# A new order for the first eight periods of an attention kernel: its second period's first scores in two more PSUM banks, seventeen dummy transposes left out

## The chip, the cores and the metric

The kernel runs on one core of one Trainium2 chip. The metric is the device time of one execution in microseconds (us); lower is better. Times are medians of several runs. The engines are TensorE (PE, with its weight loads shown apart as PEld), VectorE (DVE), ScalarE (ACT), GpSimd (POOL) and SyncE (SP), which issues every DMA of the kernel. Each engine takes its instructions strictly in the order in which the program lists them; between engines, semaphores say when data is ready or a buffer is free.

## The reference, cut to what matters

The kernel computes three things in a row: attention with a mask, a mixing layer, and an MLP. Only the start of the attention is touched by what follows.

```
q_bits = (einsum('bhsd,dk->bhsk', q, proj) > 0)      # 6 bits per token and head
k_bits = (einsum('bhsd,dk->bhsk', k, proj) > 0)
mask   = q_bucket[..., :, None] == k_bucket[..., None, :]   # buckets: the bits as a number
scores = where(mask, scale * q @ k.T, -1e9)
attn   = exp(scores - max); attn = attn / (sum(attn) + 1e-9)
x      = attn @ v                                   # 2 x 8 heads, 768 tokens, 64 per head
# then: theta = x @ w_theta; token mixing; channel mixing; norm; MLP with 4 x 512 columns
```

Everything is float32. Each operand of a product is split into a high part, rounded to the narrower fp32r form, and a low part, the rest; a product is then high by high, low by high and high by low.

## The kernel before

**Periods.** The attention has 16 heads of 768 tokens. A head's 768 query rows are six blocks of 128. The work goes in 48 periods of two row blocks: period p, block i (0 or 1) belongs to head (2p+i)//6, so head 0 is periods 0 to 2, head 1 is periods 3 to 5, and so on. One block's scores are a 128 x 772 tile `s` that fills two PSUM banks (two halves of 386 columns). In one period, with the letters that the order is written in:

- S (`s_mm`, L332): the scores of one block, four matmuls of 386 columns from the stacked tiles `tq`, `tk` (high parts, and the low parts below them) and `tq2`, `tk2` (high by low, with the bits of the mask as 7 more rows). For periods 0 to 2 there is no stack yet, and D (`direct_mm`, L503, six matmuls) and Q (`direct_bits`, L515, two) do the same from the split tiles themselves.
- M (`s_max`, DVE L340) takes the row maximum, E (`s_exp`, ACT L356) the exponential with its sum, tb (POOL L347) and R2 (DVE L363) what the norm needs, n (`s_norm`, POOL L367) normalizes into `pn`.
- U (`p_transpose`, PE L380): twelve 128 x 128 transposes, in three PSUM banks T0, T1, T2. H (`p_hi`, ACT L389) and L (`p_lo`, DVE L101) split them into `pth` and `ptl`.
- PV (`pv_mm`, PE L405): twelve matmuls into bank O; O and X (ACT L414, DVE) take the result out.

**PSUM.** There are eight banks: T0, T1, T2 and O, one each, and S0 and S1, two each. Block 0 of every period uses S0, block 1 uses S1. So D of period 1, block 0, waits until E of period 0, block 0 has read S0.

**Bits.** ac, ay, ab, aw make the mask bits of the first pair of heads; bc (PE L286, six matmuls of 384 columns), by (ACT L304), bb (DVE L310), bw make those of the next three pairs, in four chunks that use T2 and O in turn.

**Loads and splits.** SP loads the raw k and q of a pair of heads (lr, L166), v (lv, L174, the tile `vs`) and `gT` (gl, L654), and copies split tiles into the stacks of a head (sk, six DMAs, L248 to L253; sb, two for the bits, L647, L648). ACT splits off high parts (sh: `hik`, `hiq`, L210), DVE and POOL low parts (sl: `lok`, `loq`). vh (ACT L94) makes the high part of `vs` in two halves, into `vv`; vl the low part. At most eight of SP's DMAs are under way: the trace shows SP's issue of one waiting for the DMA issued eight places earlier.

**Dummies.** `warm` is a tile that nobody reads. Twelve matmuls of 384 columns write it at the start (L549), and seventeen transposes of the identity (L493) between the scores of period 0 and those of period 1.

**What sets the order.** The text `head` lists the operations of the first eight periods one by one; from period 8 on, the tables `plan` and `plan_b` and the dictionaries `bg`, `bg2`, `bg3` (background work by period) make the order. An operation's place in that list is its place on its engine. So one engine does not see how far the others have come, except where it waits for them.

Of the kernel before, what the change touches and what calls it, by code (L numbers as in the profile page):

```python
# [9 lines left out]
F32 = mybir.dt.float32  # L10
# [5 lines left out]
PSUM = bass.MemoryType.PSUM  # L16
# [17 lines left out]
def attn_moe_kernel(  # L34
# [35 lines left out]

    def bank(tag, name):
        return psum.tile([128, 512], F32, tag=tag, name=name)
# [360 lines left out]
    def theta_steps(c, x, y):  # L433

        r = slice(256 * x, 256 * x + 256)
        o = {}

        def s():
            if "h" not in WA:
                WA["h"] = const.tile([128, 4, 512], F32R, tag="wAh", name="thh")  # L440
                WA["l"] = const.tile([128, 4, 512], F32R, tag="wAl", name="thl")
            o["t"] = conv_tiles(ap_, th_st[c, x])
            conv_s(*o["t"])

        return (
            (at, 0, s), (at2, y, lambda: conv_y(*o["t"])), (at3, 1, lambda: conv_low(*o["t"])),
            (at3, 1 + y, lambda: conv_join(*o["t"])), (at2, 1 + y, lambda: cast(act, WA["h"][:, c, r], o["t"][1])),
            (at, 2 + y, lambda: sub(pool, WA["l"][:, c, r], o["t"][1], WA["h"][:, c, r])),
        )

    order.enter_context(tc.manual_schedule())

    plan = (
        ("Sa", 0), ("U0", 2), ("L2", 3), ("nb", 2), ("Ma", 0), ("H0", 2), ("X", 4), ("D", 0),
        ("R2", 1), ("U1", 2), ("Sb", 0), ("Mb", 0), ("H1", 2), ("U2", 2), ("Ea", 0), ("ta", 0), ("H2", 2),
        ("G", 0), ("na", 1), ("PV", 3), ("tb", 0), ("Eb", 0), ("L0", 2), ("C", 0), ("L1", 2), ("O", 3),
    )

    plan_b = (
        ("Sa", 0), ("B1", 2), ("L2", 3), ("B2", 2), ("U0", 2), ("Ma", 0), ("H0", 2), ("B3", 2),  # L460
        ("Sb", 0), ("ta", 0), ("nb", 2), ("X", 4), ("R2", 1), ("Ea", 0), ("Mb", 0), ("U2", 2), ("G", 0),
        ("U1", 2), ("H1", 2), ("H2", 2), ("L0", 2), ("C", 0), ("PV", 3), ("L1", 2), ("na", 1), ("B4", 2),
        ("Eb", 0), ("O", 3), ("tb", 0),
    )

# [29 lines left out]
    def direct_mm(p, i):  # L495

        ps = psum.tile([128, 2, 512], F32, tag=f"S{i}", name=f"s{p}_{i}")
        s_ps[p, i] = ps
        r = slice((2 * p + i) * 128, (2 * p + i + 1) * 128)
        K, kk = (64, [hl["k", 0, y] for y in (0, 1)]) if p == 0 else (128, kz)  # L500
        for x, y in ((0, 0), (0, 1), (1, 0)):
            for hf in range(2):
                pe.matmul(  # L503
                    ps[:, hf, 0:HW], hl["q", 0, x][0:K, r],
                    kk[y][0:K, hf, :], start=(x + y == 0), stop=False,
                )
# [41 lines left out]
    for x in range(12):  # L548
# [5 lines left out]
    TS = tuple(range(22, 46, 3))  # L554
    bg, bg2, bg3 = {}, {}, {}

    def at(step, fn, *args):
        bg.setdefault(step, []).append((fn, args))

    def at2(step, fn, *args):  # L560
        bg2.setdefault(step, []).append((fn, args))

    def at3(step, fn, *args):
        bg3.setdefault(step, []).append((fn, args))


    for h in range(5, B * H):
        at({8: 20}.get(h, 3 * h - 7), stack_dma, h)
        at({8: 21, 9: 21}.get(h, 3 * h - 7), stack_bits, h)
    v_steps = {2: (6, 9, 10), 3: (15, 16, 18), 4: (20, 22, 23)}  # L570
    for n in range(2, NPAIR):
        ld, *hi = v_steps.get(n, (6 * n - 6, 6 * n - 3, 6 * n - 2))
        at(ld, load_v, n)
        for x in range(2):
            at2(hi[x], v_hi, n, act, x)
            at(hi[x] + 1, v_lo, n, pool, x)
    for n, ld in ((6, 8), (7, 13)):
        at(ld, load_raw, n)
    for nm, n, *hi in (
        ("k", 5, 7, 11), ("q", 5, 8, 9), ("k", 6, 12, 13), ("k", 7, 14, 15),  # L580
        ("q", 6, 16, 17), ("q", 7, 17, 18),
    ):
        for x in range(2):
            at2(hi[x], split_hi, nm, n, act, x)
            at(hi[x] + 1, split_lo, nm, n, pool, x)
    for i in range(8):
        c, x = divmod(i, 2)
        at(TS[i] - 2 if i < 2 else max(TS[i] - 3, TS[i - 2] + 2), theta_load, c, x)
        for slot, d, fn in theta_steps(c, x, int(i < 7)):
            slot(TS[i] + d, fn)  # L590
# [18 lines left out]
    for step, fn, j, a in (  # L609
        (30, z_hi, 0, 0), (31, z_hi, 0, 1), (32, z_lo, 0, 0), (32, z_lo, 0, 1),  # L610
        (33, z_hi, 1, 0), (36, z_hi, 1, 1), (37, z_lo, 1, 0), (38, z_lo, 1, 1),
        (38, z_hi, 2, 0), (39, z_hi, 2, 1), (43, z_lo, 2, 0), (44, z_lo, 2, 1),
    ):
        at(step, fn, j, a)
# [3 lines left out]

    def run_bg(q):
        def run(p):  # L620
            for fn, args in q.pop(p, []):
                fn(*args)
        return run

    ops = {
        "Sa": lambda p: s_mm(p, 0), "Sb": lambda p: s_mm(p, 1),
        "Ma": lambda p: s_max(p, 0), "Mb": lambda p: s_max(p, 1),
        "ta": lambda p: None, "tb": s_lone,
        "Ea": lambda p: s_exp(p, 0), "Eb": lambda p: s_exp(p, 1),
        "R2": s_recip, "na": lambda p: s_norm(p, 0), "nb": lambda p: s_norm(p, 1),  # L630
        "B1": lambda p: bits_chunk(*bq[p], "T1"), "B2": lambda p: bits_y_(*bq[p]),
        "B3": lambda p: bits_b_(*bq[p]), "B4": lambda p: bits_p_(*bq[p]),
        "PV": pv_mm, "O": pv_evac_a, "X": pv_evac_b,
    }
    for u in range(3):
        ops[f"U{u}"] = lambda p, u=u: p_transpose(p, u)
        ops[f"H{u}"] = lambda p, u=u: p_hi(p, u)
        ops[f"L{u}"] = lambda p, u=u: p_lo(p, u)
    K0 = 8
    nxt = {op: K0 - d for op, d in plan}  # L640

# [11 lines left out]
    def g_load():  # L653
        sp.dma_start(out=gT, in_=g_ln.rearrange("(c p) -> p c", p=128))  # L654

# [6 lines left out]
    def bp_(x, e):  # L662
# [9 lines left out]
    hops = dict(  # L672
# [11 lines left out]
        n=s_norm, U=p_transpose, H=p_hi, L=p_lo, PV=pv_mm, O=pv_evac_a, X=pv_evac_b,  # L684
    )

    head = """
        sh.k.0.0.0 pb.0.0 pb.0.2 sl.k.0.0.0 pb.0.1 sh.k.0.1.0 sl.k.0.1.0 sh.q.0.0.0 sl.q.0.0.0 sh.q.0.1.0 ac.0
        sl.q.0.1.0 fk ac.1 ay.0 ay.1 kz.1.1 ac.2 ay.2 D.0.0 ab.0 lr.3.0 ab.1 ac.3 sh.k.1.2.0 D.0.1 ay.3 ab.2
        sh.q.1.2.0 aw.0.1 aw.1.1 pb.1.0 aw.2.0 kz.0.0 ab.3 Q.0.0 M.0.0 Q.0.1 warm.17 pb.1.2 E.0.0 lr.3.1 M.0.1  # L690
        sl.q.1.2.1 E.0.1 pb.1.1 D.1.0 sl.k.1.2.0 sh.k.3.2.0 Q.1.0 tb.0 lr.2.0 R2.0 lr.2.1 aw.3.0 M.1.0 n.0.1
        sk.1 sh.k.2.2.0 D.1.1 n.0.0 E.1.0 U.0.2 Q.1.1 U.0.0 sh.q.3.2.0 sl.k.2.2.0 sl.k.3.2.0 U.0.1 sl.q.3.2.1
        H.0.0 D.2.0 M.1.1 H.0.2 bc.0.1 L.0.2 L.0.0 Q.2.0 sh.q.2.2.0 E.1.1 M.2.0 by.0 tb.1 H.0.1 bc.1.0 D.2.1
        lv.0 bb.0 sl.q.2.2.1 L.0.1 by.1 sb.1 R2.1 Q.2.1 bw.0.1 n.1.0 E.2.0 bb.1 vh.0.0 lr.4.0 bc.3.1 M.2.1
        vh.0.1 S.3.0 lr.5.0 vl.0.0.0 bc.2.0 by.3 bw.1.1 E.2.1 U.1.0 by.2 M.3.0 S.3.1 bb.3 n.1.1 U.1.1 E.3.0
        vl.0.1.1 R2.2 bb.2 U.1.2 tb.2 bw.3.1 H.1.0 M.3.1 n.2.0 H.1.1 S.4.0 PV.0 H.1.2 E.3.1 L.1.0 L.1.1 lr.4.1
        M.4.0 tb.3 R2.3 sh.k.4.0.0 gl U.2.0 n.2.1 O.0 n.3.0 bw.2.1 L.1.2 X.0 S.4.1 sl.k.4.0.1 U.2.1 E.4.0 U.2.2
        H.2.0 M.4.1 H.2.1 sk.2 H.2.2 E.4.1 S.5.0 lv.1 sh.q.4.0.0 PV.1 lr.5.1 L.2.0 sb.2 L.2.1 M.5.0 L.2.2 R2.4
        O.1 tb.4 X.1 n.3.1 sh.k.4.1.1 E.5.0 U.3.0 S.5.1 U.3.2 U.3.1 n.4.1 H.3.0 H.3.2 H.3.1 S.6.0 M.5.1 sk.4
        n.4.0 L.3.0 vh.1.0 L.3.2 PV.2 E.5.1 L.3.1 sl.q.4.0.1 U.4.2 O.2 vh.1.1 M.6.0 sk.3 R2.5 X.2 vl.1.0.1  # L700
        U.4.0 sb.3 S.6.1 tb.5 H.4.0 sl.k.4.1.0 sb.4 U.4.1 H.4.2 M.6.1 n.5.0 E.6.0 H.4.1 L.4.0 E.6.1 PV.3 n.5.1
        S.7.0 U.5.0 sh.q.4.1.0 O.3 L.4.2 L.4.1 M.7.0 H.5.0 U.5.2 S.7.1 X.3 R2.6 tb.6 U.5.1 E.7.0 H.5.1 H.5.2
        M.7.1 PV.4 vl.1.1.1 L.5.0 sl.q.4.1.1 n.6.0 E.7.1 tb.7 O.4 L.5.1
    """

    for w in head.split():
        op, *args = w.split(".")
        hops[op](*(int(x) if x.isdigit() else x for x in args))

    steps = [(k, plan_b if k - 2 in bq else plan) for k in range(K0, NPER)]  # L710
    for k, now in steps:
        for op, d in now:
            if op == "G":
                run_bg(bg)(k - 2)
            elif op == "C":
                run_bg(bg2)(k - 2)
            elif op == "D":
                run_bg(bg3)(k - 2)
            elif op[0] == "B":
# [764 lines left out]
```

## Time and profile before

| | before |
|---|---|
| median of 3 runs | 664.55 us |
| lowest and highest run | 663.78 and 665.03 us |
| span of the profiled execution | 662.6 us |
| PE busy | 657.1 us, 99% of the span |
| DVE busy | 557.5 us, 84% |
| ACT busy | 416.4 us, 63% |
| POOL busy | 310.5 us, 47% |

The span runs from the first instruction to the last in the profiled execution; the measured time of a run has some 1.95 us more around it (664.55 - 662.6). Busy shares are means over the whole kernel. The attention is the first third; what happens in its first 30 us or so is read from the rows of that stretch alone.

### The profile page before, as it was taken

What the parts mean: (1) busy time and instruction counts of PE and PEld (TensorE: products, weight loads), DVE (VectorE), ACT (ScalarE), POOL (GpSimd) and SP (SyncE); (2) the same over time, 40 slices, a digit from 0 to 9 for tenths busy, and PEclk for the clock granted to TensorE, in tenths of its full rate; (3) what the DMA queues carried; (4) which work ended last, traced back from release to release, by engine and by line L of the source; (5) the groups of instructions that cost most, each with busy time, mean ns of one, the idle gap of its engine ahead of it and who ended that gap; (6) DMA issues with size and microseconds to landing.
All of it is one profiled execution on the core that took longest, in us unless ns stands there. A gap on an engine that the chain in (4) does not pass through costs nothing.

```text
span 662.6 us, 11210 instructions
## 1 busy us (share of the span) xinstructions
PE 657.1 (99%) x3771; PEld 591.7 (89%) x3771; DVE 557.5 (84%) x1002; ACT 416.4 (63%) x864; POOL 310.5 (47%) x418
## 2 busy tenths in 40 slices
PE   9999999999999999999999999999999999999998
PEld 7999999999999888888888888989998999999997
DVE  6899988999999999999888889986767686867655
ACT  7899998999999896776535544553433433343321
POOL 5887887667787644233433133434150505051400
PEclk9999999999999999999999999999999999999999
DMA  8977544475540411222422122102121121211022
GB/s 248 240 176 173 135 108 114 116 172 128 127 96 0 161 51 61 80 75 95 148 81 64 48 96 65 63 1 64 64 65 66 62 96 33 97 49 46 1 80 111
DMA packets 32374, 62.24 MB, mean 94 GB/s; under 512 B 4482, under 2 KB 11732, under 8 KB 32317
## 3 DMA queue, kind: packets, MB, share of 16 engines
q1 hardware_dynamic: 32317, 61.53, 33.1%
q8 instruction: 30, 0.49, 0.3%
q14 instruction: 27, 0.22, 0.1%
HBM read 39.98 MB, written 3.15 MB: 65 GB/s over the span
## 4 chain that ended last, share of the span: by engine, by line
PE 95%; DVE 2%; DMA 1%; SPq 1%; POOL 1%; issue 0%; ACT 0%; POOLq 0%
PE o L1191 20%; PE acc L856 15%; PE o L405 9%; PE s L332 9%; PE t L380 9%; PE Z L1148 8%; PE a L898 5%; PE v L1148 5%; PE th L790 4%; PE zy L1148 2%; PE Y L1148 2%; PE bits L286 2%; PE s L503 1%; PE xt L967 1%; PE ut L883 1%; DMA tk<-bits 1%
## 5 line engine op out<-in xcount | busy, mean ns | idle before, releaser
L1191 PE MATMUL o<-arena,hh 128*128 128x512 f32 (+1 forms) x388 | 119.1, 388 | 0.0
L367 POOL TENSOR_SCALAR pn<-p,l,M 128x768 f32<-128x768 f32 x96 | 94.6, 986 | 38.8 <-DVE l L363 25.6
L340 DVE TENSOR_REDUCE M<-s 128x1 f32<-128x772 f32 x96 | 90.9, 947 | 4.1 <-PE s L515 2.0
L101 DVE TENSOR_TENSOR ptl<-t,pth 128x512 fp32r<-128x512 f32 x144 | 90.6, 678 | 1.3 <-ACT pth L389 1.0
L356 ACT ACTIVATE p<-s,M 128x772 f32<-128x772 f32 x96 | 87.5, 912 | 2.4 <-DVE M L340 2.0
L117 POOL TENSOR_SCALAR cs<-st 128x512 f32<-128x512 f32 (+2 forms) x68 | 44.8, 665 | 84.6 <-DVE cy L131 75.1
L1191 PEld LDWEIGHTS o<-arena,hh 128*128 128x128 f32 x388 | 72.1, 188 | 13.6
L389 ACT ACTIVATE pth<-t 128x512 fp32r<-128x512 f32 x144 | 81.1, 599 | 4.3 <-PE t L380 3.0
L332 PE MATMUL s<-tk,tq 128*128 128x386 f32 (+1 forms) x360 | 82.8, 351 | 0.0
L380 PE MATMUL t<-ident,pn 128*128 128x128 f32 x576 | 80.3, 273 | 0.4 <-POOL pn L367 0.4
L1191 PE MATMUL o<-arena,hl 128*128 128x512 f32 (+1 forms) x194 | 75.5, 389 | 0.0
L856 PE MATMUL acc<-arena,tokh 128*128 128x512 f32 x240 | 75.3, 395 | 0.0
L380 PEld LDWEIGHTS t<-ident,pn 128*128 128x128 f32 x576 | 68.5, 141 | 6.3 <-POOL pn L367 1.4
L1156 ACT ACTIVATE sn<-Z 128x384 f32<-128x384 f32 x39 | 19.2, 492 | 67.2 <-PE Z L1148 67.2
L332 PEld LDWEIGHTS s<-tk,tq 128*128 128x128 f32 (+1 forms) x360 | 59.4, 190 | 0.1
L856 PEld LDWEIGHTS acc<-arena,tokh 128*128 128x128 f32 x240 | 44.0, 188 | 8.5
L1198 DVE TENSOR_TENSOR U<-o,U 128x512 f32<-128x512 f32 x48 | 32.9, 689 | 21.2 <-PE o L1191 20.5
L856 PE MATMUL acc<-arena,tokl 128*128 128x512 f32 x120 | 46.9, 391 | 0.0
L405 PE MATMUL o<-pth,vv 128*128 128x256 f32 x288 | 46.0, 295 | 0.1
L131 DVE SCALAR_TENSOR_TENSOR cy<-cy,cs 128x512 uint32<-128x512 uint32 (+2 forms) x72 | 41.4, 575 | 3.6
L114 ACT ACTIVATE cy<-st 128x512 f32<-128x512 f32 (+2 forms) x72 | 39.5, 561 | 7.8 <-DVE tokl L101 2.5
L125 DVE SCALAR_TENSOR_TENSOR cs<-st,cs 128x512 uint32<-128x512 uint32 (+2 forms) x76 | 44.1, 580 | 0.2
(260 smaller groups left out, 1481.8 us busy)
## 6 DMA issues: line engine op xcount, KB each, us to landing
st<-in_w_dram SPq DMA_DIRECT2D x36, 256.0 KB
st<-in_w_dram SPq DMA_DIRECT2D x14, 512.0 KB
tk<-hik SPq DMA_DIRECT2D x30, 193.0 KB
tq<-hiq SPq DMA_DIRECT2D x30, 192.0 KB
st<-in_wrT_dram SPq DMA_DIRECT2D x12, 384.0 KB
st<-in_wiT_dram SPq DMA_DIRECT2D x12, 384.0 KB
vs<-in_v_dram SPq DMA_DIRECT2D x8, 384.0 KB
tk<-lok SPq DMA_DIRECT2D x15, 193.0 KB
```

The source lines that it names most:

```text
L101: eng.tensor_tensor(out=o, in0=i, in1=f(hi), op=ALU.subtract)
L117: eng.tensor_scalar(out=s, in0=f(t)[:, :, 1], scalar1=0.0, scalar2=1.0, op0=ALU.mult, op1=ALU.mult)
L332: pe.matmul(ps[:, hf, 0:HW], lt[0:K, x * 128:(x + 1) * 128], rt[0:K, hf, :], start=(K == 128), stop=(K != 128),)
L340: vec.tensor_reduce(out=m_t[p][:, 0, i:i + 1], in_=s_ps[p, i][:, :, 0:HW], axis=AX.XY, op=ALU.max, negate=True)
L356: act.activation(pt, ps[:, :, 0:HW], AF.Exp, bias=m[:, 0, i:i + 1], accum_out=l_t[p][:, 0, i:i + 1])
L367: pool.tensor_scalar(out=pn.rearrange("p (h c) s -> p h (c s)", h=2), in0=p_t.pop((p, i))[:, :, 0:HALF], scalar1=l_t[p][:, 1, i:i + 1], sc ...
L380: pe.transpose(ps[:, w * 128:(w + 1) * 128], pn_t[p, i][:, c, :], ident)
L389: act.activation(ph, t_ps[p, u], AF.Copy)
L405: pe.matmul(ps, vv[:, c, e].rearrange("p a d -> p (a d)"), x[:, c::NI, :], start=(k == 0), stop=(k == 2 * NI - 1),)
L856: pe.matmul(acc, w[:, x, t * 128:(t + 1) * 128], z[:, x, y, :], start=(j == 0 and k == 0), stop=(j == NI - 1 and k == 5),)
L1148: pe.matmul(ps_t[r, b], W1[g][y][:, w, d, :], XB[s][x][:, z, d, :], start=(first == 1 and k == 0), stop=(k == 5), skip_group_check=True,)
L1191: pe.matmul(ps, lt[:, i * 128:(i + 1) * 128], W2[g][:, y, x, n], start=(k == 0), stop=(k == 5))
```

## The change

The order of the whole attention is now one long text; `plan`, `plan_b` and the dictionaries go. From about period 9 on each engine's instructions come in the same order as before. The texts of the later stages (`tail`, `half1`, `trans`) are written in another way too, and each engine's order is the same there. What differs is the first eight periods, and three things besides:

```diff
+    xpool = [xctx[0].enter_context(tc.tile_pool(name="psx0", bufs=1, space=PSUM, reuse_waits="tile"))]
...
+    def s_pair(p, i):
+        if (p, i) == (1, 0):
+            return next_pool(1).tile([128, 2, 512], F32, tag="S2", name=f"s{p}_{i}")
+        return psum.tile([128, 2, 512], F32, tag=f"S{i}", name=f"s{p}_{i}")
+
     def bank(tag, name):
-        return psum.tile([128, 512], F32, tag=tag, name=name)
+        if tag not in ("T2", "O"):
+            return psum.tile([128, 512], F32, tag=tag, name=name)
+        n = len(xpool) - 1
+        return next_pool(2 if n == 1 else n).tile([128, 512], F32, tag=tag, name=name)
...
     def direct_mm(p, i):
 
-        ps = psum.tile([128, 2, 512], F32, tag=f"S{i}", name=f"s{p}_{i}")
+        ps = s_pair(p, i)
...
-    for x in range(12):
+    for x in range(9):
...
-        aw.2.0 kz.0.0 ab.3 Q.0.0 M.0.0 Q.0.1 warm.17 pb.1.2 E.0.0
+        aw.0.1 fk aw.1.1 kz.1.1 Q.0.0 Q.0.1 sl.q.1.2.1
+        M.0.0 D.1.0 E.0.0
```

(The lines of the order are pieces of longer ones.) The banks T2 and O come from three pools in turn that lie on the same two banks: the first holds two chunks of the first bits, then the second holds `S2`, the scores of period 1, block 0, over both banks, then the third holds T2 and O for the rest of the kernel. Period 1, block 0 then no longer uses S0. The seventeen dummy transposes go, and three of the twelve dummy matmuls. All other instructions are the same in kind and number.

PE before, from the end of period 0's scores on (`s_0_165` and `s_1_182` are period 0, `s_0_232` and `s_1_265` period 1, `t` are transposes of period 0):

```order
L515 MATMUL s_0_165<-bk_99,bits 128x386 x2
L515 MATMUL s_1_182<-bk_99,bits 128x386 x2
L493 MATMUL warm<-ident 128x128 x17
L503 MATMUL s_0_232<-tkz,hiq_82 128x386 x2
L503 MATMUL s_0_232<-tk2z,hiq_82 128x386 x2
L503 MATMUL s_0_232<-tkz,loq_83 128x386 x2
L515 MATMUL s_0_232<-bk_99,bits 128x386 x2
L503 MATMUL s_1_265<-tkz,hiq_82 128x386 x2
L503 MATMUL s_1_265<-tk2z,hiq_82 128x386 x2
L503 MATMUL s_1_265<-tkz,loq_83 128x386 x2
L380 MATMUL t_2_277<-ident,pn_1_251 128x128 x4
```

PE now, the same place (`s_0_196` and `s_1_169` are period 0, `s_0_226` is period 1, block 0, in `S2`, and `s_0_247` is period 2, block 0, in S0):

```order
L525 MATMUL s_0_196<-bk_102,bits 128x386 x2
L525 MATMUL s_1_169<-bk_102,bits 128x386 x2
L513 MATMUL s_0_226<-tkz,hiq_85 128x386 x2
L513 MATMUL s_0_226<-tk2z,hiq_85 128x386 x2
L513 MATMUL s_0_226<-tkz,loq_86 128x386 x2
L525 MATMUL s_0_226<-bk_102,bits 128x386 x2
L513 MATMUL s_0_247<-tkz,hiq_85 128x386 x2
L513 MATMUL s_0_247<-tk2z,hiq_85 128x386 x2
L513 MATMUL s_0_247<-tkz,loq_86 128x386 x2
L513 MATMUL s_1_261<-tkz,hiq_85 128x386 x2
L513 MATMUL s_1_261<-tk2z,hiq_85 128x386 x2
```

The scores of period 1, block 0 follow those of period 0 without the dummies, and the scores of period 2, block 0 stand ahead of those of period 1, block 1. They are the ones that now wait for E of period 0, block 0.

ACT before, from E of period 1, block 1 (`p_1_326`) to the first H of period 1:

```order
L356 ACTIVATE p_1_326,l_274<-s_1_265,M 128x772
L304 ACTIVATE by<-bits 64x384
L389 ACTIVATE pth_300<-t_1_294 128x512
L304 ACTIVATE by<-bits 64x384
L356 ACTIVATE p_0_364,l_363<-s_0_303,M 128x772
L94 ACTIVATE vv_368<-vs_347 128x6x64 x2
L304 ACTIVATE by<-bits 64x384
L356 ACTIVATE p_1_397,l_363<-s_1_340,M 128x772
L304 ACTIVATE by<-bits 64x384
L356 ACTIVATE p_0_422,l_421<-s_0_380,M 128x772
L389 ACTIVATE pth_435<-t_0_399 128x512
```

ACT now, the same place (`p_1_332` is E of period 1, block 1; `p_0_364` and `p_1_392` are period 2; `hik_366` and `hiq_383` are halves of the fifth pair of heads):

```order
L375 ACTIVATE p_1_332,l_274<-s_1_261,M 128x772
L323 ACTIVATE by<-bits 64x384
L113 ACTIVATE vv_346<-vs_238 128x6x64
L323 ACTIVATE by<-bits 64x384
L113 ACTIVATE vv_346<-vs_238 128x6x64
L375 ACTIVATE p_0_364,l_363<-s_0_247,M 128x772
L229 ACTIVATE hik_366<-raws 128x384
L229 ACTIVATE hiq_383<-raws 128x384
L375 ACTIVATE p_1_392,l_363<-s_1_348,M 128x772
L323 ACTIVATE by<-bits 64x384 x2
L375 ACTIVATE p_0_419,l_418<-s_0_386,M 128x772
```

The two halves of `vv` move from behind E of period 2, block 0 to ahead of it, and two splits of the fifth pair come between that E and the next; before, the first of them stood behind E of period 3, block 1, the second behind E of period 4, block 1.

SP before, from the load of `vs` on (the loads L166 with `raws` are, in this order, k of the fifth pair, k of the sixth, q of the fifth):

```order
L174 DMA vs_347<-in_v_dram 128x6x128
L647 DMA tk_256<-bk_99 7x772
L648 DMA tq_254<-bits 7x2x384
L166 DMA raws<-in_kT_dram 128x768 x2
L166 DMA raws<-in_qT_dram 128x768
L654 DMA gT<-in_g_ln_dram 128x4x1
L248 DMA tq_515<-hiq_86 64x768
```

SP now, the same place:

```order
L193 DMA vs_238<-in_v_dram 128x6x128
L591 DMA tk_187<-bk_102 7x772
L592 DMA tq_185<-bits 7x2x384
L185 DMA raws<-in_kT_dram 128x768
L185 DMA raws<-in_qT_dram 128x768
L267 DMA tq_287<-hiq_89 64x768
L268 DMA tk_289<-hik_87 64x772
```

The load of q of the fifth pair comes one place earlier; k of the sixth pair and `gT` go to later periods. The twenty DMAs up to and including `vs` are the same, in the same order.

## Rows read from the trace of the kernel before

**Rows 1.** The page: span, busy time of the engines, granted clock in 40 slices.

```profile
span 662.6 us, 11210 instructions
...
PE 657.1 (99%) x3771; PEld 591.7 (89%) x3771; DVE 557.5 (84%) x1002; ACT 416.4 (63%) x864; POOL 310.5 (47%) x418
...
PEclk9999999999999999999999999999999999999999
```

**Rows 2.** Windows: stretch, us, busy of PE, PEld, DVE, ACT, POOL, clock, DMA share, GB/s.

```profile
16.00:20.00 4.00, 4.00 (x25) 3.42 (x24) 3.66 (x5) 3.90 (x8) 2.47 (x4) 1.00 1.12 205
20.00:24.00 4.00, 4.00 (x21) 3.25 (x21) 3.28 (x6) 3.47 (x8) 3.41 (x4) 1.00 1.08 329
...
28.00:46.00 18.00, 18.00 (x140) 17.70 (x139) 17.56 (x31) 17.59 (x39) 16.22 (x24) 1.00 0.88 197
```

**Rows 3.** PE in order of time: start, us, engine, line, what, count.

```profile
1.30 4.00 PE L549 MATMUL warm<-pb_lo 128*128 128x384 f32 x12 [1.30 <-DVE pb_lo L545]
...
10.70 2.08 PE L493 MATMUL warm<-ident 128*128 128x128 f32 x17
12.56 0.62 PE L503 MATMUL s<-tkz,hiq 128*128 128x386 f32 x2
...
24.14 0.34 PE L286 MATMUL bits<-loq,pb_lo 128*128 128x384 f32 x1
24.31 0.87 PE L332 MATMUL s<-tk,tq 128*128 128x386 f32 x4
25.02 0.34 PE L286 MATMUL bits<-hiq,pb_hi 128*128 128x384 f32 x1
...
26.07 0.60 PE L380 MATMUL t<-ident,pn 128*128 128x128 f32 x4
26.43 0.97 PE L332 MATMUL s<-tk,tq 128*128 128x386 f32 x4
...
27.23 1.04 PE L380 MATMUL t<-ident,pn 128*128 128x128 f32 x8
28.03 0.96 PE L332 MATMUL s<-tk,tq 128*128 128x386 f32 x4
```

**Rows 4.** The same view of ACT.

```profile
11.52 0.91 ACT L356 ACTIVATE p<-s,M 128x772 f32<-128x772 f32 x1 [0.94 <-DVE M L340]
...
20.10 0.49 ACT L304 ACTIVATE by<-bits 64x384 f32<-64x384 f32 x1
20.61 0.60 ACT L389 ACTIVATE pth<-t 128x512 fp32r<-128x512 f32 x1
21.65 0.49 ACT L304 ACTIVATE by<-bits 64x384 f32<-64x384 f32 x1 [0.44 <-PE bits L286]
22.16 0.91 ACT L356 ACTIVATE p<-s,M 128x772 f32<-128x772 f32 x1
...
23.06 0.93 ACT L94 ACTIVATE vv<-vs 128x384 fp32r<-128x384 f32 x2
...
25.09 0.91 ACT L356 ACTIVATE p<-s,M 128x772 f32<-128x772 f32 x1
...
30.05 0.55 ACT L210 ACTIVATE hik<-raws 128x384 fp32r<-128x384 f32 x1
```

**Rows 5.** The same view of SP's DMA issues, from the issue of `vs` on.

```profile
14.13 0.66 SPq L174 DMA_DIRECT2D vs<-in_v_dram  x1
...
22.00 0.50 SPq L249 DMA_DIRECT2D tk<-hik  x1
...
25.68 0.54 SPq L253 DMA_DIRECT2D tk<-lok  x1
27.38 0.39 SPq L174 DMA_DIRECT2D vs<-in_v_dram  x1
```

**Rows 6.** SP's waits between 19 and 30: line, waited for, us, times, longest.

```profile
SPq L174 <- DMA raws<-in_qT_dram: 1.1, 1, 1.1
...
SPq L249 <- DMA vs<-in_v_dram: 0.7, 1, 0.7
```

## What the change should do to the time

> **What bounds the kernel now.** I read the page first: PE is busy 657.1 of 662.6 us, so the kernel is as long as PE's work plus the few gaps in it [rows 1]. Then the windows, since only the first eight periods change: from 16 to 24 us and from 28 to 46 us PE has no gap at all, and the DMA engines stand at a share of 1.12 and 1.08 in the first of these stretches, so they are full too [rows 2]. A time can only be won here in two ways: PE work that goes, with what follows coming up behind it, or nothing. It is lost by every gap that opens on PE. From 28 us on PE stays full in either order, with the same instructions, so whatever the start of one late instruction there is moved by, the end is moved by. I follow the first scores made from the stacks, period 3, block 0 (24.31 in [rows 3]) and the first of period 4 (28.03), and ask when they start in the new order.
>
> **The dummies.** The seventeen transposes start at 10.70, the next scores at 12.56: 1.86 us of PE [rows 3]. They hid a wait. The scores that follow needed S0, which E of period 0, block 0 read until 11.52 + 0.91 = 12.43; 0.13 us later they start [rows 3, 4]. With `S2` these scores need no E any more and follow directly; the scores of period 2, block 0 take over the wait for S0, and by then PE has done 1.3 us of other work. So the most that the change can give is 1.86 us: 664.55 - 1.86 = 662.7. The wait of `S2` for the readers of the first bits' chunks (a DVE step of the first period) comes ahead of the bits that period 0 itself needs, so I price it at nothing; cover for it is those same bits. The three dummies at the start, 0.333 us each (4.00 for twelve), would let the first bits start up to 1.0 us sooner if nothing else held them; the splits of the first loads do, and what is left of it goes the way of the 1.86, below. PSUM in three pools adds waits for T2 and O at the first transposes of period 0, which wait for the norm on POOL anyway.
>
> **The splits of `vs`.** Here I find the wait that decides. ACT now lists the two halves of `vv` ahead of E of period 2, block 0, with a `by` between them; before, they stood behind it. When does `vs` land? SP issues it at 14.13, and SP's issue eight places later waits 0.7 us for it and gets through at 22.00 [rows 5, 6]. So `vs` lands at about 22.0, nearly 8 us after its issue, in a queue that is full. In the old order that cost nothing: ACT came to `vv` at 23.06 [rows 4]. In the new order ACT comes to it earlier. Even if nothing on ACT came sooner than before, E, `by` and the last H would end at about 20.10 + 0.51 + 0.55 = 21.2; with PE's lead I make it 19.7. Any of these is ahead of 22.0, so the result is the same: ACT stands for `vs`. Queued behind on ACT is E of period 2, block 0, and behind that, on PE, the scores of period 3, block 0, which need the S0 that this E reads.
>
> The sum from there, with durations of [rows 4]: two halves of `vv` 0.93, the `by` between them 0.51 (21.65 to 22.16), so E starts at 22.0 + 1.44 = 23.4 where it started at 22.16. It ends at 24.35, and with the 0.13 from above the scores of period 3, block 0 start at 24.44, against 24.31. PE, which reached this point some 1.8 us early, has given it all back in one gap, about from 22.5 to 24.4. **The step from E:** ACT goes on with 0.90 of E, then a half of `hik` and a half of `hiq` at 0.55 or a little less (the row at 30.05), so E of period 2, block 1 starts at 25.4 instead of 25.09, and the scores of period 3, block 1, can start at 25.4 + 0.91 + 0.13 = 26.4. PE has by then done the scores (0.71, 24.31 to 25.02) and a chunk of bits (1.05, 25.02 to 26.07): 24.44 + 1.76 = 26.2, so it waits 0.2. Then the scores (26.43 to 27.23: 0.80), and three groups of transposes (0.36 and 0.80, from 26.07 to 26.43 and 27.23 to 28.03): 26.4 + 1.96 = 28.36 for the first scores of period 4, against 28.03 [rows 3]. The shift is +0.3. ACT's splits of the fifth pair are then behind it, which frees about 1 us of ACT between 30 and 45, where PE has no gap to give back. So the time is 662.6 + 0.3 + 1.95 around the span = 664.85; the profiled execution with what lies around it is the median of the runs. I take **664.8**, which is no change that can be measured: about 0.2%, 1.3 us, is what a measurement of this kernel can tell, so faster means under 663.2 and slower over 665.9. `vs` may land 0.5 us to either side; the case's own range is 664.3 to 665.6.
>
> **The loads that move.** `gT` and k of the sixth pair leave the queue's busy stretch, and the stacks of the third head come sooner. Nobody in the first thirty us waits for these, and period 6, which needs that stack, had it in time; worth nothing. None of it is ahead of `vs`: the twenty DMAs up to it keep their order, which is why I don't let it land sooner.
>
> **Rivals.** *Faster: ACT isn't held.* If `vs` landed by 20 us, the lead of the dummies would reach the scores of period 3: 662.7 to 663.0. It shows as faster if `vs` comes by about 20.3. For it: in the new order the work of PE and DVE ahead of it comes earlier, and with it possibly SP's issues. Against it: a DMA share over 1 from 16 to 24 [rows 2], the same bytes in the same order ahead, and an issue at 14.13 that was already nearly 8 us ahead of the landing, so that an earlier issue only waits longer. Chance 0.18, with what I have misread in the walk on this side.
>
> *Slower: q of the fifth pair.* A half of `hiq` of the fifth pair now stands on ACT between the two E of period 2; ACT comes to it at 23.4 + 0.90 + 0.55 = 24.85. Its load comes one place earlier than before. Where it stood, it landed at 27.38: the SP issue eight places later waited 1.1 us for it [rows 5, 6]. In the new place, that of k of the sixth pair, the load was in by 25.68, when the issue eight places behind that one went out without waiting for it [rows 5]. With a landing at L the first scores of period 4 start at L + 0.55 + 0.91 + 0.13 + 1.96 = L + 3.55, so the shift is L - 24.48: at 25.68 it is 1.2, or 665.75, still no change; at 27.38 it is 2.9, or 667.4. It is slower from a landing at 25.8 on. Against it, `gT` no longer stands behind this load. The Trainium skill ("DMA: Bandwidth & Descriptors", Specifications) says that transfers under 512 bytes fall below the line rate; `gT` goes in pieces of 4 bytes, and by that rule its going would make the late landing of 27.38 less likely; no row here parts the two. Chance 0.09.
>
> *Slower: TensorE's clock.* The granted clock is full in all slices [rows 1], yet the twelve dummies at the very start take 4.00 us, 0.333 each, against 0.17 for a matmul of the same 384 columns at 24.14: the pace of 1.2 GHz, then of 2.4 [rows 3]. Before the first row PE had done nothing. After it PE never stood for long in this trace, and now it stands 0.9 us at about 12 and 1.9 us ahead of 24.4. If the clock fell in the second gap and the next work ran as the dummies did, that is 12 x (0.333 - 0.17) = 2.0 us more: 666.8. The Trainium skill ("TensorE: Matmul & The Clock Gate", Part 1) says that the clock follows how busy TensorE has lately been and falls to 1.2 GHz when it idles; by that rule leaving dummies out can cost more than they did. Nothing in this trace shows a fall after a gap of 2 us. Chance 0.07.
>
> **How the numbers follow.** No change that can be measured 0.66, at 664.8; faster 0.18, around 662.9; slower 0.16, at 665.9 to 667.4 by either rival. To hold 8 in 10 the range takes in nearly all of the faster case and the near end of the slower ones: 662.7 to 666.0.
>
> **What would show it.** In the new profile ACT should stand idle for about 2 us ahead of the first `vv`, released by a DMA at about 22.0; E of period 2, block 0 at 23.4; a gap of nearly 2 us on PE, ended by that E, with the scores of period 3 at 24.4; period 4 at about 28.3; and PE full from there to 46. The scores of period 1 should start at 10 to 10.5 without waiting for an E. If the scores of period 3 start at 22.5 to 23.5, my landing time of `vs` is wrong and the kernel is faster. If E of period 2, block 1 starts behind 26, it is the load of q; if the matmuls behind the gap are 0.33 apart, it is the clock.

## The result: 670.6 us, slower by 0.8%

| | before | after |
|---|---|---|
| median of 5 runs | 664.54 us | 670.62 us |
| lowest and highest | 663.78 and 665.03 | 667.45 and 671.92 |
| ratio, 95% interval | | 1.0082 (1.0062 to 1.0102) |
| span of the profiled execution | 662.6 us | 668.8 us |
| PE busy | 657.1 us | 661.8 us |

The kernel became slower by 6.1 us, outside the range of the forecast. PE has twenty instructions fewer and is busy 4.7 us longer; the page says so in two lines (busy us, share of the span, instructions), and its row for the granted clock is full as in [rows 1]:

```profile
span 668.8 us, 11162 instructions
...
PE 661.8 (99%) x3751; PEld 594.4 (89%) x3751; DVE 556.6 (83%) x1002; ACT 417.5 (62%) x864; POOL 312.8 (47%) x418
...
PEclk9999999999999999999999999999999999999999
```

Fewer instructions and more busy time: the instructions themselves got longer. PE in order of time shows where (start, us, line, what, count; in brackets the idle time ahead and what ended it):

```profile
1.30 3.25 PE L559 MATMUL warm<-pb_lo 128*128 128x384 f32 x9 [1.30 <-DVE pb_lo L555]
4.61 0.69 PE L305 MATMUL bits<-hik,pb_hi 128*128 128x384 f32 x1
6.13 0.69 PE L305 MATMUL bits<-lok,pb_lo 128*128 128x384 f32 x1 [0.84 <-ACT pb_lo L113]
6.62 0.52 PE L305 MATMUL bits<-hik,pb_hi 128*128 128x384 f32 x1
6.94 0.52 PE L305 MATMUL bits<-lok,pb_lo 128*128 128x384 f32 x1
...
14.40 1.01 PE L513 MATMUL s<-tkz,hiq 128*128 128x386 f32 x2
15.21 0.85 PE L513 MATMUL s<-tk2z,hiq 128*128 128x386 f32 x2
...
19.67 0.85 PE L513 MATMUL s<-tkz,hiq 128*128 128x386 f32 x2
20.31 0.58 PE L513 MATMUL s<-tk2z,hiq 128*128 128x386 f32 x2
20.73 0.51 PE L513 MATMUL s<-tkz,loq 128*128 128x386 f32 x2
...
28.66 0.87 PE L351 MATMUL s<-tk,tq 128*128 128x386 f32 x4
```

The pace is read from start to start: 6.62 to 6.94 is 0.32 us for 384 columns, 19.67 to 20.31 is 0.64 for two matmuls, and from 20.3 on it is faster: 0.21 at first (20.31 to 20.73 for two), later 0.18. 384 columns in 0.32 us is 1.2 GHz. In the kernel before that pace ends with the dummies of [rows 3]; here it lasts until 20.3. Some 40 matmuls run in it, 0.145 us longer each than at 0.175, which is 5.8 us by estimate. The lead of the seventeen transposes that are gone, 1.86 us, is set against that; the first bits start 0.76 us earlier (4.61 against 5.37), and a wait of 0.84 follows. Together that makes 4.0 us; the scores of period 3 start at 28.66 instead of 24.31, which is 4.35.

ACT's wait for `vs`, on which the forecast rested, is not there, because everything came so late that `vs` had landed (ACT, same view):

```profile
25.25 0.49 ACT L323 ACTIVATE by<-bits 64x384 f32<-64x384 f32 x1
25.64 0.51 ACT L113 ACTIVATE vv<-vs 128x384 fp32r<-128x384 f32 x1
```

From there the shift grows: the first PV starts 4.6 us later than before (33.45 against 28.83), the one of period 20 6.8 us later (124.7 against 118.0). Those last 2 us are small waits, the largest (0.98 us) for the norm on POOL at 91 us. In the whole span 6.2 us are left.

### The profile page after: what moved, and what is told of

The parts are those of the page before. It is cut to its first block, busy times and chain, and to the rows that moved or that the text cites. A ratio compares the mean times of both kernels' runs of the same rounds, so it can differ in the third digit from the quotient of the medians.

```text
span 668.8 us, 11162 instructions
## 1 busy us (share of the span) xinstructions
PE 661.8 (99%) x3751; PEld 594.4 (89%) x3751; DVE 556.6 (83%) x1002; ACT 417.5 (62%) x864; POOL 312.8 (47%) x418
## 4 chain that ended last, share of the span: by engine, by line
PE 91%; DMA 4%; POOL 2%; SPq 1%; issue 1%; ACT 1%; DVE 0%; POOLq 0%
PE o L1192 20%; PE acc L857 15%; PE o L424 9%; PE t L399 8%; PE s L351 8%; PE Z L1149 8%; PE a L899 5%; PE th L791 5%; PE v L1149 5%; PE zy L1149 2%; PE Y L1149 2%; DMA tk<-hik 2%; DMA tk<-lok 1%; POOL pn L386 1%; PE bits L305 1%; PE ut L884 1%
## 5 line engine op out<-in xcount | busy, mean ns | idle before, releaser
L1199 DVE TENSOR_TENSOR U<-o,U 128x512 f32<-128x512 f32 x48 | 32.9, 689 | 21.3 <-PE o L1192 20.5
```

## The experiments

Fourteen kernels were run besides these two. Their medians come with the kernel before run beside them on the same chip (664.5 to 664.9 us). "Twelve" and "seventeen" are the two sets of dummies.

| kernel | what | median us | lowest, highest, runs | ratio to before, 95% |
|---|---|---|---|---|
| after | the change | 670.62 | 667.45, 671.92, 5 | 1.0062 to 1.0102 |
| a12 | after, twelve | 666.70 | 664.94, 668.93, 7 | 1.0018 to 1.0053 |
| a_w17 | after, seventeen | 668.95 | 666.28, 671.41, 7 | 1.0045 to 1.0092 |
| a9_pb | after, pb_lo earlier | 667.35 | 665.96, 673.23, 12 | 1.0032 to 1.0070 |
| a12_d0 | a12, bits between the scores | 667.33 | 665.89, 669.01, 6 | 1.0024 to 1.0056 |
| a12_d0_vh | a12_d0, vv later | 667.58 | 666.21, 670.69, 6 | 1.0031 to 1.0072 |
| a12_w17 | after, twelve and seventeen | 668.06 | 667.08, 672.34, 6 | 1.0042 to 1.0084 |
| a12_d0_w17 | a12_d0, seventeen | 668.00 | 665.76, 670.70, 8 | 1.0031 to 1.0065 |
| a12_d0_w17_vhq | and no load waits on ACT | 666.48 | 665.98, 667.62, 5 | 1.0022 to 1.0050 |
| b9 | before, nine | 664.27 | 663.32, 669.45, 12 | 0.9984 to 1.0023 |
| b_no17 | before, no seventeen | 668.10 | 667.04, 669.81, 6 | 1.0040 to 1.0074 |
| b_s2 | before, banks, no seventeen | 667.97 | 665.58, 669.22, 6 | 1.0029 to 1.0064 |
| b_s2_w17 | before, banks alone | 665.70 | 664.25, 667.43, 11 | 1.0002 to 1.0021 |
| b_s2_m6 | before, banks, six wide dummies | 667.03 | 665.60, 668.57, 6 | 1.0024 to 1.0051 |
| b_vhq | before, load waits alone | 665.10 | 664.46, 667.12, 11 | 1.0005 to 1.0024 |

### What ends the slow pace at the start: a12, a_w17, a9_pb, b9

```diff
# a12
-    for x in range(9):
+    for x in range(12):
# a_w17
-        kz.1.1 Q.0.0 Q.0.1 sl.q.1.2.1
+        kz.1.1 Q.0.0 Q.0.1 warm.17 sl.q.1.2.1
# a9_pb
-        pb.0.0 sh.k.0.1.0 pb.0.1 pb.0.2 sh.q.0.0.0
+        pb.0.0 pb.0.2 sh.k.0.1.0 pb.0.1 sh.q.0.0.0
# b9 (the kernel before)
-    for x in range(12):
+    for x in range(9):
```

> The changed kernel with twelve dummy matmuls at the start again instead of nine; the seventeen transposes stay out. Theory 1 (the three dummies at the start decide when TensorE leaves 1.2 GHz): the 386-column matmuls of period 0 are 0.18 us apart instead of 0.32, the first scores of period 3 start at about 24.4 instead of 28.7, and the time is 664 to 666 us. Theory 2 (the gap of 0.84 us behind the first bits matmul, which pb_lo's place on ACT opens, decides): the gap is still there, the pace stays 0.32 and the time 668 to 672. Theory 3 (the seventeen transposes decide): as theory 2, 668 to 672.

> The changed kernel with the seventeen dummy transposes again behind the bits of period 0's scores; nine dummies at the start. Theory 3 (the seventeen decide the clock): the pace rises to 0.18 us behind them, at about 16 us, and the time falls by 1 to 3 us to 667 to 669. Theories 1 and 2: they come too late, the pace stays 0.32 until about 20, and 17 transposes at half pace add 2 to 3 us: 671 to 675.

> The changed kernel with nine dummies, and on ACT pb_lo again ahead of the second half of hik, as in the kernel before. Theory 2 (the gap of 0.84 us behind the first bits matmul decides): with the gap gone or moved the pace rises to 0.18 us by about 6 us and the time is 664 to 666. Theory 1 (the number of dummies decides): the pace stays 0.32 us and the time 667 to 672.

> The kernel before with nine dummy matmuls at the start instead of twelve, everything else as it was. Theory 1: the pace of the first bits and scores is 0.32 us, it rises much later than at 4.7, and the time is 667 to 671. Theories 2 and 3: no gap on PE of more than some tenths opens and the seventeen transposes are there, so the pace rises as before and the time stays 664 to 665.

With twelve dummies the slow pace is over at the first bits, and the median falls by 3.9 us. The gap of 0.84 us is gone as well, because the dummies now last until 5.5 us; so this run alone doesn't part theory 1 from theory 2. But the slow pace comes back, which no theory had said, and the time stays 0.7 us above the 664 to 666 of theory 1. PE of a12, and its windows (stretch, us, busy of PE, PEld, DVE, ACT, POOL, granted clock, DMA share, GB/s):

```profile
1.30 4.21 PE L559 MATMUL warm<-pb_lo 128*128 128x384 f32 x12 [1.30 <-DVE pb_lo L555]
5.57 0.68 PE L305 MATMUL bits<-hik,pb_hi 128*128 128x384 f32 x1
6.06 0.36 PE L305 MATMUL bits<-lok,pb_lo 128*128 128x384 f32 x1
...
13.43 1.01 PE L513 MATMUL s<-tkz,hiq 128*128 128x386 f32 x2 [0.77 <-ACT p L375]
...
16.17 0.60 PE L513 MATMUL s<-tk2z,hiq 128*128 128x386 f32 x2
```

```profile
10.00:13.00 3.00, 2.66 (x12) 1.83 (x12) 2.69 (x4) 2.98 (x6) 2.91 (x5) 0.99 0.99 317
13.00:16.00 3.00, 2.57 (x8) 2.57 (x9) 2.33 (x5) 3.00 (x7) 1.72 (x5) 0.50 1.06 263
16.00:20.00 4.00, 4.00 (x26) 3.50 (x25) 2.72 (x5) 2.70 (x6) 2.37 (x4) 0.96 1.11 209
```

From 13 to 16 us the granted clock is 0.50: the lower level. What PE did ahead of it: the scores of period 0, the four bits matmuls, the scores of period 1, and a gap of 0.77 us in which it waited for E of period 0, block 0.

The nine dummies leave the start to chance. Of four profiles with nine, the slow pace lasts until 20.3 in the changed kernel and until 20.5 in a9_pb, where the gap of 0.84 us is closed; it ends by about 5 in a_w17 (with a gap of 0.41) and by 6.6 in b9. With twelve it ends by 7.5 in every profile (the latest is b_vhq). So a slow start without the gap is shown, against theory 2. But theory 1 doesn't hold as it stands either. b9 has nine dummies in the old order, and its median, 664.27, is what theories 2 and 3 expected: ten of its twelve runs lie between 663.3 and 665.5, two at 669.3 and 669.5. Those two have no profile, so that they are the long slow start is argued and not shown; their mean granted clock reads 1.000, as that of the changed kernel's profiled run does. And a9_pb, which differs from the changed kernel in the place of pb_lo alone, has a median 3.3 us lower, though the two intervals still overlap at their ends (1.0062 to 1.0070); nine of its twelve runs lie below 668.5, and the profile is of one of the slow ones (670.9). So nine dummies let the slow start happen, and the gap may make it more frequent. What the three dummies and what the gap cost by themselves these runs don't part: none has the gap with twelve.

In a_w17 the seventeen transposes are there, and the clock falls all the same, while they run (17 in 3.42 us, where [rows 3] has 2.08). Its 668.95 lies in the range of theory 3, but what happened is neither of the two mechanisms expected:

```profile
10.62 3.42 PE L503 MATMUL warm<-ident 128*128 128x128 f32 x17
```

### What the seventeen transposes did: b_no17

```diff
-        Q.0.0 M.0.0 Q.0.1 warm.17 pb.1.2
+        Q.0.0 M.0.0 Q.0.1 pb.1.2
```

> The kernel before without its seventeen dummy transposes, twelve dummies at the start. Theory 'clock' (the work between 10.7 and 12.6 us keeps TensorE at 2.4 GHz): PE stands 1.7 us for E of period 0, block 0, the 386-column matmuls behind it are 0.32 us apart, and the time is 665.5 to 667.5. Rival (the transposes only fill a wait): the scores of period 1 start at 12.6 as before at 0.18 us apart, and the time stays 664 to 665.

This takes the transposes out of the kernel before and nothing else. It costs 3.4 us, all six runs above 667, where 665.5 to 667.5 was expected. PE, and the windows of the kernel before, then of b_no17:

```profile
12.62 1.01 PE L503 MATMUL s<-tkz,hiq 128*128 128x386 f32 x2 [1.80 <-ACT p L356]
13.43 0.85 PE L503 MATMUL s<-tk2z,hiq 128*128 128x386 f32 x2
```

```profile
10.00:13.00 3.00, 3.00 (x23) 2.72 (x23) 2.55 (x4) 2.06 (x6) 2.15 (x4) 1.00 0.99 331
13.00:16.00 3.00, 3.00 (x18) 2.36 (x16) 2.47 (x5) 2.32 (x5) 2.14 (x5) 1.00 1.07 240
```

```profile
10.00:13.00 3.00, 1.20 (x5) 0.88 (x6) 2.49 (x4) 2.23 (x6) 2.13 (x4) 0.86 1.00 355
13.00:16.00 3.00, 3.00 (x9) 2.12 (x9) 1.12 (x4) 1.92 (x4) 2.13 (x5) 0.50 1.06 217
16.00:20.00 4.00, 4.00 (x17) 3.33 (x18) 3.03 (x4) 1.73 (x3) 1.23 (x1) 0.63 1.11 237
```

The transposes did not only fill a wait. PE stands 1.80 us in their place, as I had read, and the scores of period 1 start at 12.62, as before (12.56). But in the gap the clock falls to 0.50, the matmuls behind it are 0.32 us apart until 18.9, and the first PV is 2.8 us late. It is so in every run: the mean granted clock of the six is 0.989 to 0.995, that of the eleven runs of the kernel before beside them 0.997 to 1.000. The Trainium skill ("TensorE: Matmul & The Clock Gate", Part 1) says that the clock falls to 1.2 GHz when TensorE idles; the trace of b_no17 agrees, with the fall at about 12.2 us in the gap. In b_s2 below the clock falls without a gap, so idling is not the whole of it.

### The banks alone, and a shorter filling: b_s2, b_s2_w17, b_s2_m6

The pools in turn, as in the change, go into the kernel before (`bank`, `next_pool`, `s_pair`, `direct_mm`), and then:

```diff
# b_s2
-        Q.0.1 warm.17 pb.1.2
+        Q.0.1 pb.1.2
# b_s2_m6 (wide: 384 columns of hik by itself, into T0)
-        Q.0.1 warm.17 pb.1.2
+        Q.0.1 wide.6 pb.1.2
```

> The kernel before in its own order, with the scores of period 1, block 0 in the two banks of T2 and O by the three pools, and without the seventeen dummies; twelve dummies at the start. One part of the change alone: ACT's two halves of vv stay behind E of period 2, block 0. If the clock holds, the scores of period 1 start at 10.8, those of period 3 at 22.5 to 23.2, and the time is 662.7 to 663.8. If the clock falls between 10 and 13 us as in the last runs of the changed order, the lead goes into the slow stretch: 665 to 667.

> The kernel before with the two PSUM banks for the scores of period 1, block 0, and all its dummies. The banks alone: the dummies end where E of period 0, block 0 ends, so nothing moves; the time is 664 to 665, within 0.2% of before. Rival (the pools in turn add waits for T2 and O): 665.5 to 667.

> The kernel before with the two PSUM banks, and six matmuls of 384 columns that nobody reads in place of the seventeen transposes: about 1.05 us of PE instead of 1.86. If the clock holds, the scores of period 1 start at 11.8 instead of 12.6 and up to 0.8 us reach the scores of period 3: 663.7 to 664.6. If six don't hold it, 0.32 us apart behind them and 666 to 668.

The banks alone cost 0.1% in the old order, through a wait that I had named in the prediction and priced at nothing. The transposes of period 0 write T2 first there, which now has to wait until E of period 1, block 0 has read `S2` (PE of b_s2_w17):

```profile
17.11 0.63 PE L399 MATMUL t<-ident,pn 128*128 128x128 f32 x4 [0.97 <-ACT p L375]
```

In the changed order those transposes come later, and a12_d0 shows no such wait.

Without the dummies, PE does go straight on (the scores of period 1 at 11.29), and the clock falls at about 11 us without a gap ahead (PE and windows of b_s2):

```profile
11.29 1.01 PE L522 MATMUL s<-tkz,hiq 128*128 128x386 f32 x2
```

```profile
10.00:13.00 3.00, 2.95 (x10) 2.34 (x10) 2.61 (x5) 2.46 (x7) 2.31 (x4) 0.67 1.02 347
13.00:16.00 3.00, 3.00 (x9) 2.12 (x9) 2.88 (x6) 2.72 (x5) 2.75 (x4) 0.50 1.06 245
```

The lead ends in the slow stretch, as the second half of the expectation said; its 665 to 667 was too low for the 667.97 measured. Six wide dummies, 1.05 us at the fast pace, don't hold the clock either: they take 1.93 us, the clock falling while they run, in this profile, and the median is 667.0.

```profile
10.89 1.93 PE L518 MATMUL warm<-hik 128*128 128x384 f32 x6
```

Over all profiles: with the seventeen transposes the granted clock is full from 10 to 20 us in seven of eight (a_w17 is the exception). Without them it falls there in five of the six that had left the slow pace of the start by then (a12_d0 is the exception).

### ACT and the loads, in the changed order: a12_d0, a12_d0_vh

```diff
# a12_d0 = a12 and
-        sl.q.0.1.0 ac.3 ay.2 ab.0 lr.3.1 D.0.1 ay.1
+        sl.q.0.1.0 ay.2 ab.0 lr.3.1 D.0.1 ac.3 ay.1
# a12_d0_vh = a12_d0 and
-        by.0 R2.1 M.2.0 vh.0.0 D.2.1 bb.0 by.1 vh.0.1 Q.2.1 L.0.1 E.2.0
+        by.0 R2.1 M.2.0 D.2.1 bb.0 by.1 Q.2.1 L.0.1 E.2.0 vh.0.0 vh.0.1
```

> The changed kernel with twelve dummies and the last chunk of the first bits between the two blocks of period 0's scores, as in the kernel before, instead of ahead of both. Theory 'order' (two blocks of 64-row scores back to back let the clock fall at 10 to 13 us): the pace stays 0.18 us, PE then stands for ACT at 22.5 to 24.3 (vv waits for vs), the scores of period 3 start at 24.4 and the time is 664.5 to 666. Rival (something else lets it fall, or chance): 0.32 us apart from 13 to 16 us again, 666 to 668.

> As the run before it, and ACT's two halves of vv behind E of period 2, block 0, as in the kernel before. If ACT's wait for vs costs what I said, and the clock holds: E of period 2, block 0 starts by 21.8, the scores of period 3 at 22.6 to 23.2, 1.2 to 1.8 us ahead of the run before it, and the time is lower by 1 to 1.8 us. If the clock falls, PE reaches the scores of period 3 only at 24.5 and the two runs agree within 0.5 us.

The profile of a12_d0 kept its clock full up to 46 us, so it shows the changed order as the forecast had it. ACT first, then PE:

```profile
22.20 0.53 ACT L113 ACTIVATE vv<-vs 128x384 fp32r<-128x384 f32 x1 [2.09 <-DMA vs<-in_v_dram]
...
23.54 0.90 ACT L375 ACTIVATE p<-s,M 128x772 f32<-128x772 f32 x1
...
25.63 0.52 ACT L229 ACTIVATE hiq<-raws 128x384 fp32r<-128x384 f32 x1 [0.68 <-PE s L351]
```

```profile
24.59 0.98 PE L351 MATMUL s<-tk,tq 128*128 128x386 f32 x4 [1.38 <-ACT p L375]
...
27.09 0.99 PE L351 MATMUL s<-tk,tq 128*128 128x386 f32 x4 [0.47 <-ACT p L375]
```

ACT stands 2.09 us for `vs`, E of period 2, block 0 starts at 23.54 (forecast: 23.4), the scores of period 3 at 24.59 (24.44). The lead is given back in that gap on PE (1.38 us), as forecast, and the clock holds over it. What the forecast didn't have is the second gap, 0.47 us: ACT stands 0.68 us ahead of the split of q of the fifth pair. The trace puts this wait down to a matmul, but that load's last packets land at 25.52, and the split starts at 25.63. E of period 2, block 1 starts at 26.06 (forecast: 25.4), the first scores of period 4 at 29.32 (28.36), and the first PV is 1.3 us late. But the runs of this kernel have a median of 667.3, and the mean granted clock of its six runs goes down to 0.995, with three at 0.997, where the kernel before shows mostly 0.999 to 1.000: the profile caught one of the better executions (666.4). The place of the bits chunk is not what decides. In a12_d0_vh the clock fell again at 13.4 in the profile, PE reached the scores of period 3 at 24.6, and the two medians agree (667.33 and 667.58): the second case of the expectation. What `vv` costs when the clock holds is therefore not measured there.

### All dummies back, with and without ACT's load waits: a12_w17, a12_d0_w17, a12_d0_w17_vhq, b_vhq

```diff
# a12_w17 = a12, a12_d0_w17 = a12_d0, each with
-        kz.1.1 Q.0.0 Q.0.1 sl.q.1.2.1
+        kz.1.1 Q.0.0 Q.0.1 warm.17 sl.q.1.2.1
# a12_d0_w17_vhq = a12_d0_w17 and
-        vh.0.0 D.2.1 bb.0 by.1 vh.0.1 Q.2.1 L.0.1 E.2.0 sh.k.4.0.0 ... sh.q.4.0.0 bw.0.1
+        D.2.1 bb.0 by.1 Q.2.1 L.0.1 E.2.0 vh.0.0 vh.0.1 ... bw.0.1
+        ... E.3.1 sh.k.4.0.0 ... E.4.1 sh.q.4.0.0
# b_vhq (the kernel before): vh.0.0 and vh.0.1 behind by.0 and by.1, sh.k.4.0.0 and
# sh.q.4.0.0 behind E.2.0, lr.4.0 lr.4.1 in a row, lr.5.0 and gl behind lv.1
```

> The changed kernel with both sets of dummies again: twelve matmuls at the start and the seventeen transposes. Theory (the clock takes most of what the change lost): the clock stays full, the scores of period 1 start at 12.6, those of period 3 at 24.6, period 4 at 28.5 to 29, small waits later add about 1 us, and the time is 665 to 666.3. Rival (the new order itself loses it): 667 to 670.

> As the run before it, and the last chunk of the first bits between the two blocks of period 0's scores, as in the kernel before. If the place of that chunk matters for the clock, fewer of its runs are slow and its median is 0.5 to 2 us lower than that of the run before it; if not, the two agree within 0.5 us, at 665 to 666.3.

> The changed kernel with both sets of dummies, the last chunk of the first bits between period 0's scores, ACT's two halves of vv behind E of period 2, block 0, and the two splits of the fifth pair behind E of period 3, block 1 and E of period 4, block 1, as in the kernel before. Theory (what is lost beyond the dummies is ACT standing for the two loads): no gap on PE between 22 and 28, the scores of period 3 at 24 to 24.6, the first PV at 28.8 to 29.3, small waits later about 1 us; 664.8 to 666, 2 to 3 us below the run with the load waits. Rival (the rest of the new order): the time stays at 667 to 669.

> The kernel before with its order, its banks and all its dummies, but with ACT's two halves of vv ahead of E of period 2, block 0, the first splits of k and q of the fifth pair between the two E of period 2, and the loads of that pair one behind the other with k of the sixth pair and gT later. Theory: E of period 2, block 0 starts at 23.4 to 23.6 and the scores of period 3 at 24.5; ACT stands for q of the fifth pair until 24.7 to 28, which moves the first PV by 0.5 to 4 us, and in the worse cases the clock falls in the gap: 665.5 to 668. Rival (ACT's waits are hidden by PE's own work): 664.3 to 665.

With both sets of dummies the clock holds through the start in the profiles, and the time is still 668: the theory that the dummies are all of it falls. The profile of a12_w17 shows the rest. ACT, PE, and the windows:

```profile
22.64 0.52 ACT L113 ACTIVATE vv<-vs 128x384 fp32r<-128x384 f32 x1 [1.64 <-DMA vs<-in_v_dram]
...
28.17 0.52 ACT L229 ACTIVATE hiq<-raws 128x384 fp32r<-128x384 f32 x1 [2.30 <-DMA raws<-in_qT_dram]
```

```profile
25.03 0.99 PE L351 MATMUL s<-tk,tq 128*128 128x386 f32 x4 [0.95 <-ACT p L375]
...
29.63 1.66 PE L351 MATMUL s<-tk,tq 128*128 128x386 f32 x4 [2.55 <-ACT p L375]
...
31.08 2.76 PE L399 MATMUL t<-ident,pn 128*128 128x128 f32 x12
```

```profile
28.00:30.00 2.00, 0.37 (x1) 0.37 (x2) 0.17 (x1) 1.81 (x5) 0.06 (x1) 0.73 0.22 57
30.00:32.00 2.00, 2.00 (x9) 1.90 (x9) 1.71 (x3) 1.46 (x4) 2.00 (x3) 0.50 0.02 8
...
34.00:36.00 2.00, 2.00 (x10) 2.00 (x9) 0.83 (x1) 1.00 (x3) 0.32 (x1) 0.56 0.42 119
```

q of the fifth pair is awaited until 28.2. ACT stands 2.30 us, PE 2.55, and in that gap the clock falls to 0.50 and stays there up to about 35.7. Two of the forecast's rivals came together, one setting off the other, and the first PV is 6.1 us late. This profiled run is the slowest of the six (672.3); a gap of this size need not be in each. In the profile of a12_d0_w17 the clock is full up to 46 us, ACT stands 0.83 us for `vs` and 0.86 ahead of the split of q (at 26.00), and the first PV is 1.7 us late. The median of that kernel is 668.00, within 0.1 us of a12_w17: the place of the chunk doesn't matter, but both are above the 665 to 666.3 that I had written.

With the load waits gone as well (a12_d0_w17_vhq) the scores of period 3 start at 24.55, the first PV at 29.32, 0.5 us late, with no gap on PE put down to ACT, and the median is 666.5. At the first PV the two profiles, with and without the waits, are 1.2 us apart. The median is 1.5 us below that of a12_d0_w17, and its five runs lie close together (665.98 to 667.62). But the two ran at different times: against the kernel before beside each they are 3.1 and 1.9 us slower, and their intervals overlap, so in the times the gain isn't clear of noise. The lower half of what I expected (2 to 3 us) is missed, and the time is above the 664.8 to 666 that I had written. What is left, 1.9 us, is in the profile not the clock, which is full up to 46 us: the shift grows from 0.5 at the first PV to 1.0 at period 4 (45 us), 1.15 at period 6 and 1.6 at period 12; the kernel before then has a wait of its own at 90 us, and from period 20 on the shift is 1.4. From period 4 to period 12 it grows in a12_d0 too, by 0.75. In the kernels with the old order it doesn't: b_no17 is 2.8 us late at the first PV and 2.8 at period 14. So it goes with the new order of the first periods, in which some background work stands later; that this work is the cause is argued, not shown. Which step of it makes each of the small waits I did not try.

Put into the kernel before, the load waits alone (b_vhq) cost 0.5 us in the median, between the two cases of the expectation. Its profile is 1.0 us late already at the scores of period 1 (13.52 against 12.56), since the slow pace of the start lasts until 7.5 in it. E of period 2, block 0 then starts at 24.56, the scores of period 3 at 25.61, and the first PV is 2.0 us late, of which about 1.0 is due to the waits; 0.7 us is won back at 90 us, where the kernel before has a wait of 0.4 us on POOL's norm. PE's own work hides part of ACT's waits there (PE stands 0.17 and 0.32 us), and the clock is full from 10 to 46 us.

## Why the prediction was wrong

**What bounds the kernel** held in the main: what the start is late by reaches the end. But PE did not stay full from 28 us on, as I had it for either order: from 60 to 124 us it stands 1.3 us in the changed kernel and 0.4 in the kernel before, and 4.35 us at period 3 becomes 6.2 in the span.

**The dummies** were the step that failed. I priced the seventeen transposes as a filling of 1.86 us that could go, and the three at the start as 0.333 us each that would be given back. b_no17 shows the first: without them, and with the same start of period 1 to a tenth, the kernel loses 3.4 us to the clock. a12 shows the second: with twelve dummies again the median of the changed kernel is 3.9 us lower. It is not their number alone: in the old order (b9) nine cost nothing in the median, and with the gap of 0.84 us closed (a9_pb) the changed kernel's median is 3.3 us lower, at the edge of the noise. The row from which I read them was right, and it held a sign that I used only for a price: the first dummies at 0.333 us, the rest of the trace at 0.17. I asked what the clock would do after a gap ahead of 24.4, and not what had brought about that rise, nor what in the trace kept it.

**The sum for `vs`** was right as a mechanism and in size up to period 3: 2.09 us of waiting, 23.54 and 24.59, against 23.4 and 24.44, shown by a12_d0. (With its own 24.35 for the end of E the sum gives 24.48, not 24.44.) The step from there was too small: +0.3 at period 4 was 1.3 in a12_d0, because ACT waited for q of the fifth pair too, which the sum had left to a rival. In the changed kernel itself all this is hidden behind the slow start, which is more than 4 us.

**The loads that move:** "worth nothing" was too simple. Nobody waits for them in the first 30 us, but with the new order of background work the shift grows by about 1 us between 29 and 80 us (0.5 to 1.6 in a12_d0_w17_vhq). The forecast had no term for that.

**The rival on the clock** named the right thing in the wrong place. I put the fall into the gap ahead of 24.4, at 2.0 us and a chance of 0.07. It happened at the start (40 matmuls, 5.8 us) in the changed kernel, in a stretch that begins between 11 and 13.4 us in a12, a_w17, b_no17, b_s2, b_s2_m6 and a12_d0_vh, and in a12_w17 in the gap of 2.55 us behind the named one. At the named place itself a12_d0 has its gap of 1.38 us, and the clock held. The chance was far too low, since a kernel that carries instructions which nobody reads may carry them for the clock; and 12 x 0.163 was no bound, since the slow stretch lasts as long as it takes the clock to rise again: 15.7 us here, some 3 to 7 us in the others.

**The rival on q of the fifth pair** was right in mechanism, and its chance of 0.09 was too low: by the landing events of the traces the load's last packets come in behind 25.8, where this rival began, in five of the nine profiles of the changed order, at 25.9 to 28.1. In a12_w17 it is 28.1, later than the 27.38 that I had as the far end. The Trainium skill ("DMA: Bandwidth & Descriptors", Specifications) gives 512 bytes as the least transfer for the line rate. By that I had thought a late landing less likely with `gT` out of the way, and the runs don't bear it out: without `gT` behind it the load lands at 23.8 to 28.1 in ten profiles, with it at 25.4 to 27.7 in six. Its place in the queue differs too, so the two aren't parted.

**The faster rival** needed `vs` by 20.3; ACT got it at 22.2 in a12_d0 and at 22.6 in a12_w17.

## What to carry to other kernels

Before dummy instructions go, ask what clock they hold up, and where the pace of equal matmuls changes in the trace; take them out alone first, since b_no17 answers by itself what the whole change hides. A lead that is won on one engine is worth only what the next in-order engine can follow: look for each instruction that moves ahead of the critical one and waits for a load. When a change moves several things, put each alone into the old kernel: here, in the medians, leaving out the seventeen cost 3.4 us, the banks 0.8 and the loads 0.5; leaving out the three cost nothing in ten of twelve runs and some 5 us in two; and none of the parts gains.

## What the runs showed of the hardware

- The granted clock reads 1.00 at the start of a trace while the pace is that of 1.2 GHz. In the changed kernel this window shows it, at 0.32 us for 386 columns; later falls read as 0.50 (rows above). At the start the pace has to be read from the matmuls.

```profile
10.00:16.00 6.00, 6.00 (x19) 5.12 (x18) 3.12 (x6) 3.89 (x8) 3.34 (x6) 1.00 1.01 259
```

- A busy PE is not a fast one: this window has PE at 6.00 of 6.00 us, with 19 instructions where the kernel before has 41, seventeen of them the short transposes.
- The clock can fall while PE works without a gap: so it does in b_s2 (PE busy 2.95 of 3.00 us from 10 to 13, the clock at 0.67), and the seventeen transposes of a_w17 and the six wide dummies of b_s2_m6 slowed down while they ran. What in PE's work makes the difference these runs don't show. Why b_s2_m6 lost the clock where b_s2_w17 kept it was not taken further.
- With slow starts and falls, one kernel's times spread: the kernel before lies within 3.1 us over 25 runs, a9_pb within 7.3 us over twelve.
